# Earlier loads for the first two heads and a longer placing distance for attention in a fused attention and MLP kernel

## The chip, the cores and the metric

The kernel runs on one core of one Trainium2 chip. The metric is device time in microseconds (us) of one execution. Most executions of this kernel agree within a few tenths of a per cent, so differences of 1 us are near the noise.

Engines: PE is TensorE, ACT is ScalarE, DVE is VectorE, POOL is GpSimd, SP is SyncE.

## The reference

Eight batches of cosine attention (12 heads, 448 tokens, 64 per head), then a mixer: a low-rank token mix (rank 32) with a residual, and an MLP of 768 to 3072 to 768 with a residual.

```python
q_n = q / (np.linalg.norm(q, axis=-1, keepdims=True) + 1e-06)
k_n = k / (np.linalg.norm(k, axis=-1, keepdims=True) + 1e-06)
scores = np.matmul(q_n, k_n.transpose(0, 1, 3, 2)) / tau
attn = np.exp(scores - max); attn = attn / (sum + 1e-09)
x = (attn @ v), heads side by side            # [8, 448, 768]
h = x^T @ U @ V                               # over tokens, rank 32
u = x + h^T
out = u + np.maximum(u @ w_ch1, 0.0) @ w_ch2
```

## The kernel before

The kernel does not write its instructions in program order by hand. Every operation is an `Op` with an engine, a planned duration and what it depends on. A planner runs through all of them with its own clock and fixes the order on each engine. The engines then work through these orders, each in order, and wait where a semaphore says so. The order is therefore decided by what the planner believes about durations and landings, together with fixed priorities.

For PE work, the planner adds a distance to the end of what it depends on on another engine, and to the time at which a PSUM bank comes free:

```python
    SEM = 0.10
    SAFE = 0.25
...
    def ready_at(self, op, eng):
        t = 0.0
        for d in op.deps:
            ...
            if d.by == eng:
                t = max(t, d.start if eng == "PE" else d.end)
            else:
                t = max(t, d.end + self.SEM + (self.SAFE if eng == "PE" else 0.0))
        for s in op.acq:              # a buffer that must be free
            ...
            t = max(t, f + (self.SEM + self.SAFE if eng == "PE" else self.SEM))
```

PE takes the first operation that is ready by this, from streams in a fixed priority: transposes, batch 0's scores, attention times v, the small U and V matmuls, the other scores, and last the MLP, which fills what is left.

The loads of q and k go through POOL, which casts fp32 to bf16 on the way. All the loads below are planned to land 2.0 us after their transfer in batch 0:

```python
    def load_qk(b, h0, h1, ld=None, lo=0, uses=None):
        ld = ld or Slot(r_ld, 4 if uses is None else uses)
        ops = [load(lambda i=i, src=src: nc.gpsimd.dma_start(
            out=ld.tile[:, i, lo:lo + h1 - h0, :],
            in_=src[b, h0:h1].rearrange("h (s c) d -> s h (c d)", c=SC)),
            ..., acq=[ld], late=2.0 if b == 0 else LATE) for i, src in enumerate((q, k))]
...
    first = load_qk(0, 0, 2, uses=5)
    second = load_qk(0, 2, 4, first[0], 2)       # the same buffer
    ld, ops, _ = load_qk(0, 4, 8)
    ...
    begun = stats_first(*first[:2])              # squares, sums, 1/norm, normalized q and k
    ...
    state[0] = att(0)
```

Batch 0's first MLP starts before the token-major copy of `u` exists; six V matmuls make it on the side, each into a PSUM bank that VectorE must clear by an add, and all six are asked for at one point of the hidden loop:

```python
    def by_tokens(us, A, X):
        for i in range(3):
            for c0, c1 in ((0, CH), (CH, C)):
                mm = Slot(r_mm, 1)
                o = plan.add(Op("PE", pe_t(CH), ... V matmul ..., acq=[mm, us[i]], rel=[A]), pe_mlp)
                ... plan.add(Op("DVE", dve_t(CH), ... u = mm + X ..., deps=[o], rel=[mm, X], prio=2))
...
            if b == 0 and f == 9:
                by_tokens(us, *state["first"])
```

Of the kernel before, what the change touches and what calls it, by code (L numbers as in the profile page):

```python
# [10 lines left out]
FP = mybir.dt.float32  # L11
# [27 lines left out]


class Op:
    __slots__ = ("eng", "dur", "fn", "deps", "acq", "rel", "prio", "lat", "start", "end", "by", "seq", "fast")

    def __init__(self, eng, dur, fn, deps=(), acq=(), rel=(), prio=0, lat=0.0, fast=False):
        self.eng, self.dur, self.fn, self.prio, self.lat, self.fast = eng, dur, fn, prio, lat, fast
# [4 lines left out]
class Plan:  # L50
# [5 lines left out]
    BEGIN = {"PE": 1.0, "ACT": 2.0, "DVE": 0.9, "POOL": 1.3, "SP": 0.7}  # L56
    SEM = 0.10
    HOLD = 0.0
    SAFE = 0.25
    LAG = {"PE": 0.16, "ACT": 0.10, "DVE": 0.07, "POOL": 0.0, "SP": 0.0}  # L60

    def __init__(self):
# [7 lines left out]
        return s  # L70

    def add(self, op, stream=None):
        op.seq = self.n
        self.n += 1
        if stream is not None:
            stream.append(op)
        else:
            for e in op.eng.split("/"):
                self.loose[e].append(op)
        return op  # L80
# [5 lines that stand above are left out]
            if d.end is None:  # L86
                return None
            if d.by == eng:
                t = max(t, d.start if eng == "PE" else d.end)
            else:  # L90
                t = max(t, d.end + self.SEM + (self.SAFE if eng == "PE" else 0.0))
        new = []
        for s in op.acq:
            if s.i is not None:
                continue
            f = s.ring.free_at(new.count(s.ring))
            new.append(s.ring)
            if f is None:
                return None
            t = max(t, f + (self.SEM + self.SAFE if eng == "PE" else self.SEM))  # L100
        return t

    def run(self):
# [101 lines left out]
def kernel(  # L205
# [12 lines left out]
    nc = tc.nc  # L218

    B, H, S, D = q.shape  # L220
    C = H * D
    R = moe_U.shape[-1]
# [5 lines left out]
    SC = 4  # L228
    SCH = S // SC
# [7 lines left out]
    pool = ctx.enter_context(tc.tile_pool(name="pool", bufs=1))  # L237
# [9 lines left out]
    def ring(n, shape, dt, name, space=None):  # L247
        p = space or pool
        return Ring(n, lambda i: p.tile(shape, dt, name=name, tag=name, bufs=n))

    def fixed_ring(tiles):
# [3 lines left out]
    xn_t = fixed(3, [SCH, 12, 128], BF, "xn")  # L255
# [13 lines left out]
    r_uT = ring(1, [128, CC, 512], BF, "uT")  # L269

    w2_t = const.tile([128, NC, C], BF, name="w2_sb")
    r_relu = Ring(1, lambda i: pool.tile([128, 8 * R + S], FP, name="raw_uv", tag="relu", bufs=1)
                  if i == 0 else pool.tile([128, NC, 512], BF, name="relu", tag="relu", bufs=1))
    uv = Slot(r_relu, 3)

    def U_f():
        return uv.tile[:, 0:8 * R].rearrange("p (b t r) -> p b t r", b=2, t=4)

    def V_f():
        return uv.tile[:, 8 * R:]  # L280

    r_O = ring(3, [128, CH], FP, "O_sb")
    r_rd = ring(2, [128, 4, 1], FP, "rd")
    r_mm = ring(3, [128, 512], FP, "mm", psum)
# [48 lines left out]
    def fill(fn, n=256, prio=8, acq=(), deps=()):  # L333
        return plan.add(Op("DVE", 0.05 + n * 0.0005, fn, deps=deps, acq=acq, prio=prio))
# [49 lines left out]
# [6 lines that stand above are left out]
            (h1 - h0) * (0.31 if b else 0.35) + (1.2 if b == 0 and h0 == 4 and i == 0 else 0.0), acq=[ld], late=2.0 if b == 0 else LATE) for i, src in enumerate((q, k))]  # L390
        return ld, ops, lo

    def load_v(b, h0, h1):


        vb = v_t[b % 2]
        old = [last_av.get((b - 2, h // 2)) for h in range(h0, h1)]
        ops = []
        for hh in range(2):
            hs = slice(h0 + hh, h1, 2)  # L400
            for j in range(4):
                if j < 3:
                    lo, hi, base = 128 * j + 64 * hh, 128 * j + 64 * hh + 128, 0
                else:
                    lo, hi, base = (384, 448, 0) if hh == 0 else (0, 64, 64)
                for n, c, s0, s1 in segments(lo, hi):
                    p0 = base + n - lo
                    ops.append(load(lambda j=j, c=c, s0=s0, s1=s1, p0=p0, hs=hs:
                        nc.gpsimd.dma_start(  # L409
                            out=vb[p0:p0 + s1 - s0, hs, j, 0:D],  # L410
                            in_=v[b, hs].rearrange("h (s c) d -> c s h d", c=SC)[c, s0:s1]),
                        (s1 - s0) * (h1 - h0) * 0.001, deps=old, late=LATE if b else 2.0))
        for h in range(h0, h1):
            got[b, h, "v"] = ops
# [62 lines left out]
    def stats(b, h0, h1, ld, ops, lo, hold=()):  # L477

        pr = 0.3 + 0.03 * h0 if b == 0 else 4
        inv = Slot(r_inv, h1 - h0)  # L480
        o, _ = scales(b, h0, h1, ld, ops, lo, (0, 1), inv, pr, "DVE" if b else "ACT/DVE", hold)
        for p in range(h0 // 2, h1 // 2):
            o_ = norm(b, p, ld, lo + 2 * p - h0, inv, 2 * p - h0, {0: o, 1: o}, pr)
        return o_
# [22 lines left out]
    def norm(b, p, ld, la, inv, a, deps, pr):  # L507


        by_pe = b < PE_BATCHES  # L510
        first = b == 0 and p == 0
        xn, qkT = Slot(r_xn, 3 if first else 2 if by_pe else 1), Slot(r_qkT, 7)
        need = [xn_set[count[0] % len(xn_t)]]
        count[0] += 1

        def part(i, h0=0, h1=2):
            def fn():
                n = h1 - h0
                src = ld.tile[:, i, la + h0:la + h1, :].rearrange("p h (c d) -> p h c d", d=D)
                sc = inv.tile[:, i, a + h0:a + h1, :].unsqueeze(3).to_broadcast([SCH, n, SC, D])  # L520
                if i == 0:
                    dst = xn.tile[:, 8:12, :].rearrange("p c (h d) -> p h c d", h=2)
                else:
                    dst = xn.tile.rearrange("p b e -> p (b e)")[:, 0:9 * 128].rearrange(
                        "p (h x) -> p h x", h=2)[:, h0:h1, 0:SC * 128].rearrange(
                        "p h (c e) -> p h c e", c=SC)[:, :, :, 0:D]
                nc.vector.tensor_mul(dst, src, sc)  # L527
            return plan.add(Op("DVE", dve_t(256 * (h1 - h0)), fn, deps=need + [deps[i]], acq=[xn],
                               rel=[ld, inv], prio=pr))

        if first:
            ops = [part(0), part(1, 0, 1), part(1, 1, 2)]
            blocks = [(8, 12, ops[0]), (0, 4, ops[1]), (4, 8, ops[2])]
        else:
            ops = [part(1), part(0)]
            blocks = [(0, 8, ops[0]), (8, 12, ops[1])]
        if not by_pe:
            done = [plan.add(Op("SP", 0.1, lambda: nc.sync.dma_start_transpose(
                out=qkT.tile, in_=xn.tile.rearrange("p b e -> p (b e)")), deps=ops, acq=[qkT],
                rel=[xn], prio=0, lat=("x", 0.05 * 84, LATE)))]  # L540
        else:
            done = []
            for b0, b1, o in blocks:
                done.append(flip(
                    pe_tp, [(lambda z=z: xn.tile[:, z, :]) for z in range(b0, b1)], SCH,
                    lambda: qkT.tile, (lambda t_, x, b0=b0, b1=b1: key_tiles(t_, x, b0 // 4, b1 // 4)
                                   if b == 0 and b0 < 8 else [(t_[:, b0:b1, :], x)]),
                    [o], [qkT], [xn], 1, "ACT/DVE", 0.09 if first else 0.05, b == 0 and b0 < 8))
        got[b, p, "qkT"] = (qkT, lambda m: (done[:2] if m < 3 else done) if first else done, done)
        return ops  # L550
# [262 lines left out]
    def copy_op(op, dst, src):  # L813
        if op.by == "ACT":
            nc.scalar.copy(out=dst, in_=src)  # L815
        else:
# [1 line left out]


    xn_set = [fill(lambda t_=t_: nc.vector.memset(t_[:, 0:8, :], 0.0), 900, prio=i - 3)  # L820
              for i, t_ in enumerate(xn_t)]

    ones = 0x3F803F80

# [49 lines left out]
        last_mul.extend(muls)  # L874
        return stage0(b, X, muls)

    first = load_qk(0, 0, 2, uses=5)
    second = load_qk(0, 2, 4, first[0], 2)
    ld, ops, _ = load_qk(0, 4, 8)
    id_set = plan.add(Op("POOL", 0.8, lambda: make_identity(nc, ident)), pool_q)  # L880
    begun = stats_first(*first[:2])
    stats(0, 2, 4, *second, hold=begun)
    zf = fill(lambda: nc.vector.memset(U_f(), 0.0), 400, prio=0.1, acq=[uv], deps=begun)
    u0 = load_u(0)
    v0 = [plan.add(Op("SP", 0.45, lambda t=t: nc.sync.dma_start(out=V_f()[R * t:R * (t + 1)], in_=moe_V),
# [12 lines left out]
              plan.add(Op("POOL", 0.4, lambda: cast_u(1), deps=u1 + [z], rel=[uv]), pool_q)]  # L898
    state[0] = att(0)
    after = last_mul[-1:]  # L900
    state["first"] = prev["A"], prev["X"]
    go(1, 0, 4)
    load_w1(12, 18)
# [12 lines left out]
    for b in range(1, B):  # L916
        state[b] = att(b)
        if b + 1 < B:
            for h0, h1 in THIRDS:
                go(b + 1, h0, h1)  # L920
            load_v(b + 1, 0, 12)
    for b in range(B):
        mlp(b, *state[b])

# [39 lines left out]
```

## Time and profile before

| | before |
|---|---|
| time, median of 3 | 607.34 us |
| span of the profiled execution | 604.8 us |
| PE busy | 97% |
| first PE instruction | 7.92 us |
| last matmul run starts, lasts | 569.79, 31.27 us |

PE is so full that a table of busy shares says little. The useful reading is a ledger, which the prediction below builds with its lines: the actual start of a matmul less the unhindered time of all PE work before it is the lag that PE has gathered. Lag that grows between two points is time in which PE had nothing that it could do, or waited.

One correction to it, used from here on: a group of four small U matmuls of 384 columns takes 0.37 us in the trace, not 0.28. With this the lag of the kernel before is 19.5 us at the first long run of up-projections (start 40.6), 23.3 at 112 us and 25.0 at the last run of down-projections (start 569.8).

### The profile page before, as it was taken

How to read it: one execution, taken by the hardware profiler on the slowest of the kernel's cores; microseconds unless marked ns; L12 is line 12 of the kernel's file. 1: busy time of each engine (PE TensorE's matmuls, PEld its weight loads, DVE VectorE, ACT ScalarE, POOL GpSimd, SP SyncE). 2: the span in 40 equal slices, each digit the busy share in tenths (PEclk: the TensorE clock that was granted, in tenths of full speed). 3: DMA queues.
4: the chain of work that ended last, by engine and by line, in shares of the span. 5: the costliest groups of instructions: out<-in, count | busy, mean ns of one | idle time of the engine just before them, and what ended most of it. 6: DMA issues, size and time to landing. Idle time of an engine off the chain costs nothing.

```text
span 604.8 us, 11544 instructions
## 1 busy us (share of the span) xinstructions
PE 586.1 (97%) x4725; PEld 346.8 (57%) x4725; DVE 296.0 (49%) x714; ACT 279.5 (46%) x612; POOL 115.4 (19%) x177
## 2 busy tenths in 40 slices
PE   3899999999999999999999999999999999999997
PEld 1665666555555665666445665666545666654565
DVE  8979679989998987644711253015300210110011
ACT  6977652498782385317641077506442025014300
POOL 8246334071715326000500000000000000000000
PEclk9999999999999999999999999999999999999999
DMA  9999998999999999514902151030002110310021
GB/s 114 202 184 122 208 198 103 173 145 126 129 145 175 151 139 154 83 56 87 154 0 66 46 90 37 1 93 27 15 1 53 52 40 1 92 40 1 0 53 53
DMA packets 150164, 54.58 MB, mean 90 GB/s; under 512 B 115040, under 2 KB 150112, under 8 KB 150112
## 3 DMA queue, kind: packets, MB, share of 16 engines
q0 software_dynamic: 73344, 25.96, 38.6%
q1 hardware_dynamic: 76704, 27.86, 24.2%
q8 instruction: 37, 0.61, 0.4%
q14 instruction: 15, 0.12, 0.1%
q10 hardware_dynamic: 64, 0.02, 0.0%
HBM read 52.25 MB, written 11.01 MB: 105 GB/s over the span
## 4 chain that ended last, share of the span: by engine, by line
PE 92%; ACT 5%; DVE 2%; issue 0%; ACTq 0%
PE mm L785 36%; PE mm L751 35%; PE sc L563 9%; PE av L583 8%; ACT attn L568 3%; PE mm L675 1%; ACT qkT L815 1%; PE tp L365 1%; PE mm L640 1%; DVE ss L452 1%; PE sc L751 1%; DVE xn L527 0%; PE sc L675 0%; ACT uT L815 0%; DVE xn L820 0%
## 5 line engine op out<-in xcount | busy, mean ns | idle before, releaser
L751 PE MATMUL mm<-uT,w_sb 128*128 128x512 bf16 (+1 forms) x1134 | 236.1, 353 | 0.0
L785 PE MATMUL mm<-w_sb,relu 128*128 128x384 bf16 (+1 forms) x1368 | 233.8, 323 | 0.3 <-ACT uT L815 0.3
L568 ACT ACTIVATE attn<-sc 128x448 bf16<-128x448 f32 x336 | 161.0, 565 | 88.8 <-PE av L583 57.4
L785 PEld LDWEIGHTS <-relu 128*128 128x128 bf16 x1368 | 132.6, 98 | 86.7 <-issue 0.9
L751 PEld LDWEIGHTS <-w_sb 128*128 128x128 bf16 x1152 | 111.9, 98 | 101.1 <-issue 1.0
L774 ACT ACTIVATE relu<-mm 128x512 bf16<-128x512 f32 (+1 forms) x169 | 92.4, 547 | 149.2 <-PE mm L751 148.9
L794 DVE TENSOR_TENSOR O_sb<-mm,u_nat 128x384 f32<-128x384 f32 (+1 forms) x57 | 31.0, 547 | 227.1 <-PE mm L785 223.4
L563 PE MATMUL sc<-qkT 128*128 128x448 bf16 x336 | 103.4, 358 | 3.9 <-ACT attn L568 1.9
L583 PEld LDWEIGHTS <-attn 128*128 128x128 bf16 x1536 | 62.7, 98 | 16.0 <-DVE xn L527 0.8
L409 POOL DMA_DIRECT2D v_nat<-in_v_dram x98 | 63.2, 651 | 34.7 <-DMA w_sb<-in_moe_w_ch_dram 13.4
L583 PE MATMUL av<-v_nat,attn 128*128 128x65 bf16 x1536 | 66.6, 194 | 0.2 <-DVE X_sb L592 0.2
L452 DVE TENSOR_REDUCE ss<-sq 112x8 f32<-112x512 bf16 x96 | 63.0, 673 | 0.3
L527 DVE TENSOR_TENSOR xn<-qk_nat,inv 112x512 bf16<-112x512 bf16 (+1 forms) x97 | 62.5, 674 | 0.3
L563 PEld LDWEIGHTS <-qkT 128*128 128x128 bf16 x336 | 29.8, 98 | 24.2 <-issue 8.0
L387 POOL DMA_DIRECT2D qk_nat<-in_q_dram x25 | 17.9, 716 | 130.6 <-DVE xn L527 102.6
L592 DVE TENSOR_TENSOR X_sb<-av,rd 128x256 bf16<-128x256 f32 x96 | 40.0, 419 | 1.5
L590 DVE RECIPROCAL rd<-av 128x4 f32<-128x4 f32 x96 | 17.0, 179 | 38.2 <-PE av L583 36.7
L448 DVE TENSOR_TENSOR sq<-qk_nat 112x512 bf16<-112x512 bf16 x90 | 35.0, 408 | 0.2
L689 DVE TENSOR_TENSOR u_nat<-mm,X_sb 128x384 bf16<-128x384 f32 x36 | 19.1, 553 | 11.0 <-PE mm L675 10.8
L365 PE MATMUL tp<-ident,xn 112*128 112x112 bf16 x144 | 11.7, 226 | 10.0 <-DVE xn L527 9.5
L465 ACT ACTIVATE ln<-ss 112x32 f32<-112x32 f32 (+2 forms) x26 | 6.3, 241 | 32.7 <-DVE ss L452 32.5
L387 POOL DMA_DIRECT2D qk_nat<-in_k_dram x25 | 17.6, 703 | 5.8 <-DMA w_sb<-in_moe_w_ch_dram 5.8
(58 smaller groups left out, 160.8 us busy)
## 6 DMA issues: line engine op xcount, KB each, us to landing
qk_nat<-in_q_dram POOLq DMA_DIRECT2D x23, 224.0 KB, 5.2
qk_nat<-in_k_dram POOLq DMA_DIRECT2D x23, 224.0 KB, 6.4
w_sb<-in_moe_w_ch_dram POOLq DMA_DIRECT2D x4, 1152.0 KB, 14.3
w_sb<-in_moe_w_ch_dram POOLq DMA_DIRECT2D x8, 576.0 KB, 16.6
out_dram<-O_sb SPq DMA_DIRECT2D x15, 168.0 KB, 2.3
out_dram<-O_sb SPq DMA_DIRECT2D x16, 144.0 KB, 2.1
out_dram<-O_sb SPq DMA_DIRECT2D x16, 120.0 KB, 2.0
out_dram<-O_sb SPq DMA_DIRECT2D x16, 96.0 KB, 2.2
```

The costliest lines, as they stand in the source:

```text
L387: ops = [load(lambda i=i, src=src: nc.gpsimd.dma_start(out=ld.tile[:, i, lo:lo + h1 - h0, :], in_=src[b, h0:h1].rearrange("h (s c) d -> s ...
L409: nc.gpsimd.dma_start(out=vb[p0:p0 + s1 - s0, hs, j, 0:D], in_=v[b, hs].rearrange("h (s c) d -> c s h d", c=SC)[c, s0:s1]),
L448: nc.vector.tensor_mul(y, x, x)
L452: lambda i=i, a0=a0, a1=a1, sq=sq: nc.vector.reduce_sum(ss.tile[:, i, a0:a1, :].rearrange("p h c -> p (h c)"), sq.tile[:, 0:a1 - a0, :].re ...
L527: nc.vector.tensor_mul(dst, src, sc)
L563: nc.tensor.matmul(out=sc.tile[:, 0:S], lhsT=kT[:, 128 * m:128 * (m + 1)], rhs=qkT.tile[:, 8:12, :].rearrange("p c s -> p (c s)"), start=T ...
L568: exps[m] = plan.add(Op("ACT", act_t(S), lambda sc=sc, m=m: nc.scalar.activation(out=attn.tile[:, m, off:off + S], in_=sc.tile[:, 0:S], fu ...
L583: nc.tensor.matmul(out=av.tile[:, t, 0:D + 1], lhsT=attn.tile[:, m, 128 * t:128 * (t + 1)], rhs=v_t[b % 2][:, h, j, 0:D + 1], start=(j == ...
L592: muls.append(plan.add(Op("DVE", dve_t(256), lambda av=av, rd=rd, h=h: nc.vector.tensor_mul(X.tile[:, :, h * D:(h + 1) * D], av.tile[:, :, ...
L751: o = plan.add(Op("PE", pe_t(n), lambda cc=cc: nc.tensor.matmul(out=mm.tile[:, 0:n], lhsT=w1_sb[:, cc, f * 128:(f + 1) * 128], rhs=uT.tile ...
L774: nc.scalar.activation(out=relu.tile[:, f, 0:n], in_=mm.tile[:, 0:n], func=AF.Relu)
L785: nc.tensor.matmul(out=mm.tile[:, 0:c1 - c0], lhsT=relu.tile[:, f, i * 128:(i + 1) * 128], rhs=w2_t[:, f, c0:c1], start=(f == 0), stop=(f ...
```

## The change

The intent: the first two heads' q and k come as fp32 by the sync queue, so that POOL asks for the other heads at once; a memset of 0.48 us makes room for the first square; and for all attention from batch 1 on PE work is placed 0.8 us behind what it waits for instead of 0.25, so that small errors of the plan do not stop PE.

```diff
-    SAFE = 0.25
+    safe = 0.25
...
-        op.seq = self.n
+        op.seq, op.safe = self.n, self.safe
...
-                t = max(t, d.end + self.SEM + (self.SAFE if eng == "PE" else 0.0))
+                t = max(t, d.end + self.SEM + (op.safe if eng == "PE" else 0.0))
... (the same for PSUM banks; a wider first tile in the relu buffer; class First, which
...  gives heads 0 and 1 a place there)
     xn_set = [fill(lambda t_=t_: nc.vector.memset(t_[:, 0:8, :], 0.0), 900, prio=i - 3)
-              for i, t_ in enumerate(xn_t)]
+              for i, t_ in enumerate(xn_t[:2])]
...
-    first = load_qk(0, 0, 2, uses=5)
-    second = load_qk(0, 2, 4, first[0], 2)
+    first = lead, [plan.add(Op("SP", 0.45, lambda i=i, src=src: nc.sync.dma_start(
+        out=lead.tile[:, i], in_=src[0, 0:2].rearrange("h (s c) d -> s h (c d)", c=SC)),
+        acq=[uv], prio=-5, lat=2.5)) for i, src in enumerate((q, k))]
+    second = load_qk(0, 2, 4, uses=2)
...
+    xn_set.append(fill(lambda: nc.vector.memset(xn_t[2][:, 0:8, :], 0.0), 900, prio=0.2, deps=begun))
...
     state[0] = att(0)
     after = last_mul[-1:]
+    plan.safe = 0.8
...
+    plan.safe = 0.25
     for b in range(B):
         mlp(b, *state[b])
```

More of the change, by code (lines that the diff above doesn't have):

```diff
@@ L41 @@
 class Op:
-    __slots__ = ("eng", "dur", "fn", "deps", "acq", "rel", "prio", "lat", "start", "end", "by", "seq", "fast")
+    __slots__ = ("eng", "dur", "fn", "deps", "acq", "rel", "prio", "lat", "start", "end", "by", "seq", "fast", "safe")
     def __init__(self, eng, dur, fn, deps=(), acq=(), rel=(), prio=0, lat=0.0, fast=False):
@@ L99, in ready_at @@
                 return None
-            t = max(t, f + (self.SEM + self.SAFE if eng == "PE" else self.SEM))
+            t = max(t, f + (self.SEM + op.safe if eng == "PE" else self.SEM))
         return t
@@ L271 @@
     w2_t = const.tile([128, NC, C], BF, name="w2_sb")
-    r_relu = Ring(1, lambda i: pool.tile([128, 8 * R + S], FP, name="raw_uv", tag="relu", bufs=1)
+    r_relu = Ring(1, lambda i: pool.tile([128, 8 * R + S + 4 * SC * D], FP, name="raw_uv", tag="relu", bufs=1)
                   if i == 0 else pool.tile([128, NC, 512], BF, name="relu", tag="relu", bufs=1))
-    uv = Slot(r_relu, 3)
+    uv = Slot(r_relu, 6)
     def U_f():
@@ L279, in V_f, with tile @@
     def V_f():
-        return uv.tile[:, 8 * R:]
+        return uv.tile[:, 8 * R:8 * R + S]
+    class First:
+        slot = uv
+        @property
+        def tile(self):
+            return uv.tile[0:SCH, 8 * R + S:].rearrange("p (i h x) -> p i h x", i=2, h=2)
+    lead = First()
     r_O = ring(3, [128, CH], FP, "O_sb")
@@ L528, in part @@
             return plan.add(Op("DVE", dve_t(256 * (h1 - h0)), fn, deps=need + [deps[i]], acq=[xn],
-                               rel=[ld, inv], prio=pr))
+                               rel=[getattr(ld, "slot", ld), inv], prio=pr))
         if first:
```

## The prediction

> **What bounds the kernel now.** I read the page first, then the chain of waits in order of time, then the start of the timeline.
>
> ```profile
> PE 586.1 (97%) x4725; PEld 346.8 (57%) x4725; DVE 296.0 (49%) x714; ACT 279.5 (46%) x612; POOL 115.4 (19%) x177
> PE 92%; ACT 5%; DVE 2%; issue 0%; ACTq 0%
> ```
>
> TensorE is the bound: it is 97% busy and holds 92% of the chain. Only what is not matmul work in that chain can be won, so I list the longest of it, with four anchors of pure matmul work (columns: start, duration, what):
>
> ```profile
> 5.27 1.28 DVE ss L452 x2
> 29.07 3.49 ACT attn L568 x8
> 40.59 2.44 PE sc L751 x14
> 46.54 1.39 ACT qkT L815 x2
> 57.57 0.91 ACT qkT L815
> 99.99 1.02 ACT uT L815
> 101.05 11.86 PE mm L785 x72
> 146.38 1.42 ACT attn L568 x3
> 180.40 1.86 ACT attn L568 x4
> 222.89 2.87 ACT attn L568 x6
> 287.10 1.42 ACT attn L568 x3
> 293.60 28.06 PE mm L751 x130
> 569.79 31.27 PE mm L785 x216
> ```
>
> The chain's ACT pieces overstate the loss, because scores and matmuls still run beside them. So I keep a ledger: the order of the built program's matmuls, each at its unhindered pace in this trace. These paces are 28.06/130 = 0.216 us for a 512-column up-projection, 0.1625 for a 384-column one (130 in 21.12) and for a down-projection (48 in 7.80), 0.19 for a score, 0.032 for an attention-times-v matmul (32 in 1.02), 0.05 for a transpose. The whole order sums to 575.0 us. At each anchor the lag is actual start less summed work:
>
> - 40.6 (the first MLP's long run of up-projections; 21.1 us of work before it): lag 19.5. Of it 7.9 is the wait for the first transpose; 11.6 is lost while batch 0's attention runs, bound by VectorE and then ScalarE.
> - 101.05 (77.9 us of work): lag 23.2, so 3.7 lost in batch 1's attention.
> - 293.60 (267.8): lag 25.8, so 2.6 lost.
> - 569.79 (543.7): lag 26.1, so 0.3 lost. After it come 31.27 us of work and 3.7 us of the last add and store.
>
> So the most that a better order from batch 1 on can win is 3.7 + 2.6 + 0.3 = 6.6 us. Some of that is no wait: four small U matmuls cost about 0.09 us more than I charge, 15 groups of them 1.4 us. About 5.2 us is left. I find it in single places: after transposes near 47.2 and 58.1, where a score waits for the qkT copy (0.63 and 0.74), the uT transposes at 97 to 101 (0.48 + 0.33 + 0.49), and the four ScalarE pieces after 140 us (0.4 to 0.5 each, 1.8 together).
>
> The start, from the timeline (start, duration, engine, what, idle before and its releaser):
>
> ```profile
> 1.28 0.78 POOL L387 DMA_DIRECT2D qk_nat<-in_q_dram  x1 [0.84 <-POOLq L945]
> 4.47 0.48 DVE L820 MEMSET xn<- 112x512 uint32 x1
> 4.88 0.35 DVE L448 TENSOR_TENSOR sq<-qk_nat 112x512 bf16<-112x512 bf16 x1
> 4.93 0.63 ACT L446 ACTIVATE sq<-qk_nat 112x512 bf16<-112x512 bf16 x1 [2.91 <-DMA qk_nat<-in_k_dram]
> 7.92 0.56 PE L365 MATMUL tp<-ident,xn 112*128 112x112 bf16 x4 [7.92 <-DVE xn L527]
> ```
>
> ScalarE waits 2.91 us for the first k. VectorE does not wait: it runs memsets from 0.92 to 4.95, and its first square follows without idling. An earlier landing alone is therefore hidden by memsets.
>
> **What the Trainium skill says.** "Perfetto Trace Analysis", Identifying the Most-Contended Engine, says that matmul busy share is a poor measure of what is left. The trace agrees: 586.1 us busy hold 575.0 us of work. "VectorE: DVE Perf Modes", The perf-mode tier table, gives a two-tensor operation the 2x mode in bf16 and 1x with fp32. The trace agrees, with these two forms in the first 45 us:
>
> ```profile
> L527 DVE TENSOR_TENSOR xn<-qk_nat,inv 112x512 bf16<-112x512 bf16 x12 | 7.8, 691 | 0.1
> L448 DVE TENSOR_TENSOR sq<-qk_nat 112x512 bf16<-112x512 bf16 x10 | 3.8, 398 | 0.0
> ```
>
> The product with the fp32 inv takes 691 ns, the all-bf16 square 398. "DMA: Bandwidth & Descriptors", Specifications, gives a first-byte latency of about 1 us for loads started by GpSimd and 0.6 for the sync queue. Its section Issuing engines are not separate DMA queues says that all share 16 engines, so issuing from two saves only issue time. The trace before has no early sync-queue load; it shows 3.4 us from issue to landing for these 112 KB loads by POOL.
>
> **The change, part by part.**
>
> Load. Two POOL issues (0.78 + 0.67 us) go; the next loads of q and k, and all later ones, are issued about 1.4 us earlier. SyncE has nothing before its first load, so I put the issue near 0.9 us and landings near 3.4 (q) and 4 to 4.5 (k), estimates from the same 2 to 3.4 us that loads take to land here. One memset (0.48) moves from before the first square to after the first normalization.
>
> VectorE at the start. The memsets now end at 4.42. The square reads fp32, so it costs as the 1x product does: 0.58 instead of 0.29 in sequence. Two reduces of 0.62 end at 6.3, against 6.55. The normalization reads fp32 beside fp32 inv, 1x before and after: no change. The built order also puts the second scale-add before the first product, where before it waited 0.55 for ScalarE after it. So the first k tiles are ready near 8.8 instead of 9.44, q still near 7.8. The first transpose stays at 7.8 to 8.0.
>
> Then VectorE is given more: the q copy (0.36), the moved memset (0.48) and one half of the k copy (three copies, about 0.68), less one square (0.35) that ScalarE takes. Going on from 8.8: 0.36 + 0.27 + 0.48 + 0.68 + the old remainder of 4.5 - 0.27 - 0.35 gives pair 1's product at about 14.5 to 14.7, where it was at 13.95. The first exp comes 0.5 to 0.9 earlier (copies in parallel on two engines), but pair 1's exps stay near 18.0 (were 18.08). From there ScalarE sets the pace: 35 exps at 0.446 us are 15.6 in both; beside them before stand 1 square (0.51), three copy sets (2.7) and two small pairs (0.24), after 1 square, two sets and one single copy (2.8 in all). That saves 0.45. Against it, VectorE has two more copy sets in 16 to 30 us (1.8 us, it was 97% busy there), and ScalarE's in-order queue may wait up to 0.9 for a normalization. Sum for the start: **-0.3 us, +-1**.
>
> Distance. The number 0.8 instead of 0.25 holds for the PE work of batches 1 to 7's attention: other matmuls are put between a producer on another engine and its PE consumer. No instruction is added; the sum stays 575.0. I compared the two built orders at the paces above. A score reuses a PSUM bank of the third score before it; the work between the end of one and the start of the other is below 1.2 us in 48 of 273 cases before, in 9 after (below 0.9: 10 and 1), and the median rises from about 1.55 to 2.1. The tightest run of 12 scores has one per 0.41 to 0.55 us before, less or hardly more than an exp (0.446) with the other work of ScalarE; after it is 0.62 to 0.70. So the ScalarE backlogs at 146, 180, 223 and 287 should not build up: -1.6 of 1.8. After transposes near 47 us the next score stands 0.81 us later instead of 0.16, and at 58 us the copy has 0.57 + 0.9 us of work: -1.2 of 1.37. The uT transposes are split and mixed with down-projections: -1.0 of 1.3. From "up 384 x144" on both orders are the same, so the end costs what it did. I leave 0.2 for new waits. Sum: **-3.6 us**.
>
> Together: -3.9 of 607.34, **603.4 us**.
>
> **The rivals.**
>
> Everything in the chain goes: ACT pieces from 40 us on sum to about 14 us, so one would hope for 593. The ledger is against it, since only 6.6 us are lost there at all.
>
> The early load carries through: a 1.4 us earlier start on POOL and 0.9 us earlier exps reach the end of batch 0's attention, and with the distance this is 602. For it: copies in parallel, less ScalarE work. Against: VectorE's row of memsets, then its 97%.
>
> VectorE takes the place of the load: two more copy sets and the fp32 square delay pairs 2 to 5, costing up to 1 us, giving 604.5 to 605.
>
> The distance wins nothing, or delays attention until an MLP runs out of work: 607. For it: each dense stretch now lasts some 10 us longer, and VectorE with it. Against: 69 to 95 up-projections in a row still stand behind each attention, so none becomes the last.
>
> **Range and chances.** The distance can give 2.8 to 4.8, the start -1.3 to +1.0 around what I said, which makes 601.2 to 605.5 for 8 in 10. A 2% gain needs 12.1 us, twice what the ledger holds outside the start; a loss of 2% would need a new wait of 12 us that no order shows. Chances: 0.02 faster, 0.97 within, 0.01 slower.
>
> **What would show it.** The load right: first square of VectorE near 4.5 us and slower (about 0.6), first transpose still near 7.9, the first exp near 10.7. The start term right: the MLP's first long run near 40.3; near 39 or 42 it is wrong. The distance right: no ACT piece over 1 us in the chain after 101 us, and the lag growing by about 3 instead of 6.6 from the first MLP run to the last matmul. A score, or a first attention-times-v matmul, with TensorE idle before it at a new place would show that the distance is still too short or that ScalarE is now late for another reason. A different clock than 1.0, or missing weights at the first down-projection, would make all of it wrong.

## The result

605.34 us (604.82 to 606.38, four runs), beside 607.53 us (607.23 to 608.25, four runs) of the kernel before. The ratio is 0.9964 with a 95% interval of 0.9947 to 0.9982. Ratios here and below are the mean time of one kernel's runs over that of the other's of the same rounds, so they are not quite the ratio of the medians. The gain is real, about 2.2 us, and small: within 2%. The predicted 603.4 us asked for 3.9.

The changed kernel's profile has a span of 603.2 us; from its page the engine line and the chain:

```profile
PE 586.4 (97%) x4725; PEld 347.0 (58%) x4725; DVE 300.6 (50%) x728; ACT 276.9 (46%) x598; POOL 115.2 (19%) x175
...
PE 93%; DVE 2%; ACT 2%; POOL 1%; DMA 1%; issue 0%; ACTq 0%; POOLq 0%
```

ScalarE's share of the chain fell from 5 to 2%. That is 3 points of 600 us, or some 18 us, while the span fell by 1.6. This is the trap that the ledger is for. A share that leaves one engine goes to others: here PE has one point more, and POOL and the DMA one point each, which they did not have before.

Some pieces in the chain of waits, in order of time (start, duration, what):

```profile
9.48 5.13 DMA v_nat<-in_v_dram
...
25.34 2.50 DVE xn L536 x4
...
45.23 2.50 DVE xn L536 x4
...
51.87 0.93 DVE u_nat L734 x2
...
106.05 6.50 PE mm L794 x40
...
568.49 31.27 PE mm L794 x216
```

After 101 us no ScalarE piece is among the long ones any more: the four at 146, 180, 223 and 287 us are gone. Before that, VectorE has come into the chain, at 25 us and at 45 to 52 us. The points of POOL and the DMA are one place: up to 14.6 us the chain now follows POOL's loads and the landing of the first v, where before it followed VectorE. Experiment 6 tests what that is worth.

The ledger of both kernels, as growth of the lag:

| stretch | before | after | predicted change | measured change |
|---|---|---|---|---|
| up to the first long MLP run | 19.5 | 20.2 | -0.3 | +0.7 |
| from there to 62 us | 1.9 | 1.5 to 2.0 | -1.2 | about 0 |
| 62 to 112 us | 1.9 | 0.7 to 1.2 | -1.0 | -0.7 to -1.2 |
| 112 us to the last run | 1.7 | 0.8 | -1.6 | -0.9 |
| lag at the last run | 25.0 | 23.7 | -3.9 (with 0.2 left for new waits) | -1.3 |

The point at 62 us falls in the middle of small instructions, so it is good to 0.5 us; the sum of the two rows around it, -1.0, is sharper. After the last run, 34.7 us pass instead of 35.0. Together that is the 1.6 us of the spans.

So the distance did part of what was expected of it late in the kernel, nothing near 50 us, and the start got slower, not faster. The start first (timeline: start, duration, engine, what, idle before and what ended it):

```profile
0.74 0.39 SPq L886 DMA_DIRECT2D raw_uv<-in_q_dram  x1
...
4.28 0.63 ACT L455 ACTIVATE sq<-raw_uv 112x512 bf16<-112x512 f32 x1 [2.26 <-DMA raw_uv<-in_k_dram]
4.34 0.62 DVE L457 TENSOR_TENSOR sq<-raw_uv 112x512 bf16<-112x512 f32 x1
...
7.62 1.55 PE L374 MATMUL tp<-ident,xn 112*128 112x112 bf16 x12 [7.62 <-DVE xn L536]
...
10.62 0.63 ACT L455 ACTIVATE sq<-qk_nat 112x512 bf16<-112x512 bf16 x1 [1.14 <-DVE ss L461]
11.16 0.53 ACT L577 ACTIVATE attn<-sc 128x448 bf16<-128x448 f32 x1
```

The load came as thought (2.9 us from issue to landing for q, 3.1 for k), the square starts after the memsets and takes the longer time of fp32, the first transpose comes at 7.62 instead of 7.92 and the first exp at 11.16 instead of 11.44. The exp gains only 0.28 us, because in ScalarE's order a square stands in front of it, and that square waits 1.14 us for a reduce of VectorE. And yet the last exp of batch 0 ends at 37.85 us where it ended at 37.14. What lies between is the subject of half of the experiments.

Then the stretch at 50 to 54 us, some lines of PE, VectorE and ScalarE:

```profile
49.88 0.53 ACT L824 COPY qkT<-tp 128x448 bf16<-128x448 bf16 x1 [0.36 <-PE tp L374]
50.01 1.17 PE L730 MATMUL mm<-A_sb,V_sb 128*128 128x384 bf16 x3
50.31 0.50 ACT L783 ACTIVATE relu<-mm 128x384 bf16<-128x384 f32 x1
50.39 0.55 DVE L734 TENSOR_TENSOR u_nat<-mm,X_sb 128x384 bf16<-128x384 f32 x1
50.86 0.68 DVE L461 TENSOR_REDUCE ss<-sq 112x8 f32<-112x512 bf16 x1
...
51.78 1.02 DVE L734 TENSOR_TENSOR u_nat<-mm,X_sb 128x384 bf16<-128x384 f32 x2
52.39 0.79 PE L730 MATMUL mm<-A_sb,V_sb 128*128 128x384 bf16 x2 [0.24 <-DVE u_nat L734]
...
53.91 0.81 PE L760 MATMUL mm<-uT,w_sb 128*128 128x384 bf16 x4 [0.19 <-DVE u_nat L734]
```

Three V matmuls need 0.49 us and take 1.17 with their waits (0.16 of that is the last one's end); the fourth and fifth wait again, and so does the up-projection at 53.91. The lag grows by 1.6 us here, in two parts. The first 0.5 us are waits for ScalarE: by the semaphores in the built program the second V matmul waits for the copy at 49.88 and the third for the relu at 50.31. The kernel gives the transposes, the V matmuls and the MLP the same ring of three PSUM banks (`r_mm`), and the second V matmul is in the bank that the transposes before it filled and that this copy clears. The other 1.1 us, before the fourth and fifth V matmul and the up-projection, are waits for VectorE's adds, which have to clear banks of the ring and stand behind reduces of batch 1's statistics. Not all of it is new: before, the lag grew by 0.6 us at these V matmuls. The built orders show what has changed (runs of equal matmuls in PE's order; `tp` transposes, `sc` scores, `V` the six V matmuls):

```
before: ... tp*12 sc up ... sc up*2 V*2 sc*3 V*2 sc V sc V sc up*14 ...
after:  ... tp*8 up*11 tp*4 up*2 V*3 sc*3 tp*8 V*2 sc*2 V up*4 sc up*2 tp*4 ...
```

Before, scores stood between the V matmuls. The longer distance has moved those scores away, and what is left is V matmuls that follow each other faster than ScalarE and VectorE clear their banks.

### The profile page after: what moved, and what is told of

Same layout as the page of the kernel before. It is cut to its first block, busy times and chain, and to the rows that moved or that the text cites. A ratio compares the mean times of both kernels' runs of the same rounds, so it can differ in the third digit from the quotient of the medians.

```text
span 603.2 us, 11528 instructions
## 1 busy us (share of the span) xinstructions
PE 586.4 (97%) x4725; PEld 347.0 (58%) x4725; DVE 300.6 (50%) x728; ACT 276.9 (46%) x598; POOL 115.2 (19%) x175
## 4 chain that ended last, share of the span: by engine, by line
PE 93%; DVE 2%; ACT 2%; POOL 1%; DMA 1%; issue 0%; ACTq 0%; POOLq 0%
PE mm L794 36%; PE mm L760 35%; PE sc L572 10%; PE av L592 8%; PE mm L684 1%; PE tp L374 1%; DMA v_nat<-in_v_dram 1%; DVE xn L536 1%; PE mm L649 1%; POOL v_nat L429 1%; ACT attn L577 1%; PE sc L760 0%; POOL qk_nat L396 0%; DVE ss L461 0%; ACT qkT L824 0%
## 5 line engine op out<-in xcount | busy, mean ns | idle before, releaser
L760 PE MATMUL mm<-uT,w_sb 128*128 128x512 bf16 (+1 forms) x1134 | 241.3, 353 | 0.2 <-DVE u_nat L734 0.2
L794 PE MATMUL mm<-w_sb,relu 128*128 128x384 bf16 (+1 forms) x1368 | 231.3, 323 | 0.0
L577 ACT ACTIVATE attn<-sc 128x448 bf16<-128x448 f32 x336 | 164.6, 552 | 110.9 <-PE av L592 58.2
L783 ACT ACTIVATE relu<-mm 128x512 bf16<-128x512 f32 (+1 forms) x158 | 86.8, 549 | 129.3 <-PE mm L760 128.7
L536 DVE TENSOR_TENSOR xn<-qk_nat,inv 112x512 bf16<-112x512 bf16 x94 | 60.9, 681 | 2.4 <-DMA qkT<-xn 2.2
L457 DVE TENSOR_TENSOR sq<-qk_nat 112x512 bf16<-112x512 bf16 x87 | 33.7, 415 | 0.0
L785 DVE TENSOR_SCALAR relu<-mm 128x384 bf16<-128x384 f32 (+1 forms) x31 | 18.7, 604 | 12.8 <-PE mm L760 12.0
## 6 DMA issues: line engine op xcount, KB each, us to landing
w_sb<-in_moe_w_ch_dram POOLq DMA_DIRECT2D x4, 1152.0 KB, 14.6
```

Source lines behind the costliest of these rows:

```text
L457: nc.vector.tensor_mul(y, x, x)
L536: nc.vector.tensor_mul(dst, src, sc)
L577: exps[m] = plan.add(Op("ACT", act_t(S), lambda sc=sc, m=m: nc.scalar.activation(out=attn.tile[:, m, off:off + S], in_=sc.tile[:, 0:S], fu ...
L760: o = plan.add(Op("PE", pe_t(n), lambda cc=cc: nc.tensor.matmul(out=mm.tile[:, 0:n], lhsT=w1_sb[:, cc, f * 128:(f + 1) * 128], rhs=uT.tile ...
L783: nc.scalar.activation(out=relu.tile[:, f, 0:n], in_=mm.tile[:, 0:n], func=AF.Relu)
L794: nc.tensor.matmul(out=mm.tile[:, 0:c1 - c0], lhsT=relu.tile[:, f, i * 128:(i + 1) * 128], rhs=w2_t[:, f, c0:c1], start=(f == 0), stop=(f ...
```

## The experiments

Twelve runs, one of them the changed kernel again, all correct, each timed in four to six executions, beside nine to eleven of the kernel before on the same chip. "Lag" means the lag at the first long run of up-projections, then at the last run of down-projections.

### 1. The load alone

```diff
 (on the changed kernel)
-    plan.safe = 0.8
+    plan.safe = 0.25
```

> Only the load part (sync queue, memset moved), distance 0.25 everywhere. Theory, from the ledger of the changed kernel (lag at the first long run of up-projections 20.2 us against 19.5 before): the load part alone costs 0.7 us, so about 608.2 against 607.5 before, with that lag at 20.1 to 20.3. Rival: the start is neutral once the distance no longer depends on it (the later order takes the 0.7 back): 607.3 to 607.6. Second rival, the one of the prediction: it gains 0.3, 607.2.

Measured: 606.91 us (606.00 to 607.08), beside 606.89; ratio 0.9993 (0.9980 to 1.0006). Lag 20.2, then 24.8.

The 0.7 us at the start are there, as the theory says. In the time they do not show: after 112 us this order loses 0.7 us where the kernel before loses 1.7, with the same distance. The order between is another one, so that is a by-product. The load part by itself is worth nothing; the interval excludes a loss of the 0.7 us that I expected, and leaves a gain of up to 1.2.

### 2. The distance alone

```diff
 (on the kernel before)
     after = last_mul[-1:]
+    plan.safe = 0.8
...
+    plan.safe = 0.25
     for b in range(B):
         mlp(b, *state[b])
```

> Only the distance 0.8 for the attention of batches 1 to 7, the load as before. Theory: what the changed kernel lost at the start comes back, so 605.3 - 0.7 = 604.6 (gain 2.7 to 3.0), lag at the first long run of up-projections 19.5 and about 24.1 at the last matmul run. Rival: the two parts are not additive and it stays at 605.3. Prediction's own figure: a gain of 3.6, 603.9.

Measured: 606.30 us (605.73 to 607.68), beside 606.89; ratio 0.9988 (0.9976 to 1.0000). Lag 19.5, then 24.3.

The theory falls. With the undisturbed start, I expected 604.6; the distance alone is worth about 0.6 us. Its lag grows by 4.8 us from the first long run on, against 5.5 before and 3.5 in the changed kernel. The parts are not additive, since each edit makes the planner lay out everything after it anew. On top of the load, the distance is worth 606.91 - 605.80 = 1.1 us (the latter from experiment 5, measured in another group of runs).

### 3. The distance only from batch 2 on

```diff
         state[b] = att(b)
+        plan.safe = 0.8          # and not before the loop
         if b + 1 < B:
```

> As the kernel before, with the distance 0.8 only from batch 2's attention on. Theory: the loss of 2.95 us after 101 us falls to about 1.85 as in the changed kernel, and batch 1 keeps its 3.7: a gain of 1.1, so 606.4. Rival: the waits after 101 us stem from how batch 1 left ScalarE and do not change: 607.3. Other rival: batch 1's part of the distance is worth nothing net (its new waits at V matmuls eat it), so this does as well as distance alone, 604.6 to 605.0.

Measured: 605.74 us (605.23 to 606.51), beside 606.89; ratio 0.9978 (0.9966 to 0.9990). Lag 20.0, then 24.3; from 112 us on it grows by 0.5 us.

So the part from batch 2 on does what it was made for: 0.5 instead of 1.7 us are lost after 112 us, a gain of 1.2 in the ledger and 1.1 in the time. That is the gain of 1.1 of the theory. In batch 1 the distance brings nothing net (606.30 with it in experiment 2), which fits the last rival that I named, that the new V waits eat what it wins there, though not its 604.6 to 605.0. One more thing: the start of this kernel has the same order as the kernel before, and still its lag is 20.0 instead of 19.5. One profile differs from the next in the start.

### 4. The V matmuls apart

```diff
-            if b == 0 and f == 9:
-                by_tokens(us, *state["first"])
+            if b == 0 and f in (9, 12, 15):
+                by_tokens(us, *state["first"], (f // 3 - 3,))    # one pair at a time
```

> The changed kernel, with the six V matmuls of batch 0's tokens asked for in three pairs, three hidden blocks apart, instead of all at one point. Theory: the excess of 1.6 us that TensorE has at 50 to 54 us between these V matmuls (each waits for VectorE's add to free its PSUM bank, behind the statistics of batch 1) goes for the most part, so about 1.0 to 1.4 faster than the changed kernel, 604.1. Rival: VectorE is simply late there with everything, so the wait moves to other instructions and the time stays at 605.3.

Measured: 604.98 us (604.38 to 607.12, six executions), beside 606.89; ratio 0.9968 (0.9955 to 0.9981). Lag 23.0, then 25.9, in a profiled execution that was the slowest of the six (607.12).

From the first long run to 60 us the lag grows by 0.7 us instead of 1.5 to 1.6, so most of the V waits go. What stays is 0.5 us at the first pair, the part that waits for ScalarE. About 1 us is lost again at 100 to 107 us (the lag grows by 1.6 instead of 0.4), where batch 1's transposes and small matmuls now stand differently. Five of the six executions are at 604.4 to 605.3. Against the changed kernel (0.9964 and 0.9978 in two measurements) the difference is within the noise.

The slow execution is worth a look. Its order up to 50 us is that of the changed kernel, yet at 38 us it lags by 22.3 us instead of 19.6 (timeline, ScalarE and PE):

```profile
15.55 0.24 PE L592 MATMUL av<-v_nat,attn 128*128 128x65 bf16 x1 [1.19 <-DMA v_nat<-in_v_dram]
...
17.23 0.63 ACT L455 ACTIVATE sq<-qk_nat 112x512 bf16<-112x512 bf16 x1 [2.22 <-DMA qk_nat<-in_q_dram]
```

PE waits 1.19 us for v and ScalarE 2.22 us for the last heads' q. In the changed kernel's own profile PE waited 0.44 us at 14.33 for v, and ScalarE not at all for q. So the landing of these loads differs by more than 1 us from one execution to the next, and this start stands close behind them.

### 5. The changed kernel again

> The changed kernel once more, as the yardstick of this chip and as a second profile of its start. If the gain of 2.2 us of its first measurement holds: ratio 0.995 to 0.998, 605.0 to 605.9. If the start depends on when transfers land, the lag at the first long run of up-projections will again lie anywhere in 20 to 22.5 with the very same order (20.2 in its first profile, 22.5 in another kernel with the same start).

Measured: 605.80 us (604.95 to 606.26), beside 606.86; ratio 0.9978 (0.9965 to 0.9990). Lag 20.2, then 23.7, as in the first profile.

The two measurements, 0.9964 and 0.9978, overlap; the gain of the change is 1.1 to 2.2 us.

### 6. The first v planned later

```diff
 (on the changed kernel, the loads of batch 0's v)
-                n * (0.0055 if hs.step == 2 else 0.011)))
+                n * (0.0055 if hs.step == 2 else 0.011), late=3.5))
```

> The changed kernel, with the first v's landing planned 3.5 us after its transfer instead of 2.0; in the built order this only moves the first attention-times-v matmuls of batch 0 behind the twelve transposes of pair 1, where before 17 of them stood in front. Theory: in the changed kernel these held the transposes from 14.6 to 15.4 us until v landed, so the lag at the first long run falls from 20.2 to about 19.5 and the time by 0.7 (and by more where v lands late): ratio to before about 0.9955. Rival: VectorE, which stands in the chain from 24.7 to 30.3 us, sets the start with its additional copies: lag stays at 20.2, ratio as the changed kernel's.

Measured: 605.25 us (604.98 to 605.87), beside 606.86; ratio 0.9973 (0.9960 to 0.9985). Lag 20.3, then 23.8.

The edit did to PE what it should. The transposes of pair 1 in the changed kernel and in this one (timeline, PE):

```profile
14.33 1.25 PE L592 MATMUL av<-v_nat,attn 128*128 128x65 bf16 x15 [0.44 <-DMA v_nat<-in_v_dram]
15.39 0.94 PE L374 MATMUL tp<-ident,xn 112*128 112x112 bf16 x8
```

```profile
14.63 1.30 PE L374 MATMUL tp<-ident,xn 112*128 112x112 bf16 x12 [0.84 <-DVE xn L536]
15.73 1.97 PE L592 MATMUL av<-v_nat,attn 128*128 128x65 bf16 x32
```

The transposes come 0.76 us earlier, and the lag at the end of the start is the same. My theory falls. The exps of pair 1 began at 18.11 us here and at 18.14 there, and the second line shows why: all 32 attention-times-v matmuls stand in front of pair 1's first score in both orders. Here they come after the transposes, the score starts at 17.50, and ScalarE waits 0.95 us for it; in the changed kernel they come before and among the transposes, and the score starts at 17.65.

### 7. v and the later heads' q and k planned later

```diff
+            ..., late=(3.5 if h0 else 2.0) if b == 0 else LATE)   # q and k of heads 2 to 11
+                n * (0.0055 if hs.step == 2 else 0.011), late=3.5))
```

> As the kernel before this one, and the second and third load of q and k planned 3.5 us late too, so that ScalarE's square of the last heads stands behind pair 1's copies, not in front of them. Theory: the waits of ScalarE for the third load (0, 1.35 and 2.2 us in three profiles of this start) go; lag at the first long run 19.0 to 19.5 and a smaller spread of times; ratio to before 0.9945 to 0.9955. Rival: that wait was beside other waits, nothing more than with v alone.

Measured: 604.87 us (604.73 to 605.00), beside 606.86; ratio 0.9965 (0.9951 to 0.9979). Lag 19.6, then 23.7.

The start is back at the lag of the kernel before, and five executions lie within 0.3 us of each other instead of 1.3. Pair 1's exps begin at 18.09 as in all these starts; the last exp ends at 37.21 instead of 37.85. What is different between the two lies in ScalarE's queue, whose exps and copies from 26 us on read so, for the kernel before, the changed kernel and this one (timeline, ScalarE):

```profile
27.94 1.13 ACT L815 COPY qkT<-tp 128x672 bf16<-128x672 bf16 x3
28.84 8.30 ACT L568 ACTIVATE attn<-sc 128x448 bf16<-128x448 f32 x18
```

```profile
26.87 1.03 ACT L824 COPY qkT<-tp 128x672 bf16<-128x672 bf16 x3 [0.43 <-PE tp L374]
27.77 8.89 ACT L577 ACTIVATE attn<-sc 128x448 bf16<-128x448 f32 x19
```

```profile
28.45 1.09 ACT L824 COPY qkT<-tp 128x672 bf16<-128x672 bf16 x3
29.35 6.70 ACT L577 ACTIVATE attn<-sc 128x448 bf16<-128x448 f32 x15
```

In the changed kernel ScalarE reaches the copies of a later pair before its transposes are done, and waits 0.43 us; those transposes wait for VectorE's four products at 25.34. Then its exps come at 8.89/19 = 0.468 us instead of 0.447 (6.70/15), with short waits for scores between them. In this kernel the queue has other work first and does not wait there. Summed from start to start, the 35 exps with the waits behind them take 16.6 us in the changed kernel, and 15.5 in this one and in the kernel before. A square (0.5 us) more stands in the stretch here; the rest is the 0.6 us. It is the wait that the prediction had named as a risk ("ScalarE's in-order queue may wait up to 0.9 for a normalization") and had booked inside a sum that came out negative. Which of the two, VectorE's additional copies or ScalarE's order, one would call the cause is not separated by these runs.

### 8. A distance of 1.2

```diff
-    plan.safe = 0.8
+    plan.safe = 1.2
```

> The changed kernel with a distance of 1.2 instead of 0.8. Theory: what the distance still leaves (the lag grows by 3.5 us from the first long run to the end, by 5.5 before the change) is partly waits for ScalarE and VectorE that more room takes away: growth 2.5 to 3.0 and 0.5 to 1.0 faster than the changed kernel. Rival: what is left is the V matmuls behind VectorE at 50 to 54 us and the fixed cost of small matmuls, which no distance changes: growth 3.3 to 3.7, same time.

Measured: 618.70 us (617.34 to 619.53, four executions), beside 606.86; ratio 1.0191 (1.0174 to 1.0208). Lag 21.0, then 36.7.

Neither theory had this: 12 us slower. The ledger says where: the lag is 25.2 at 112 us and 36.0 at 131. The busy time of that stretch, for this kernel and then for the changed kernel (columns: PE, PEld, DVE, ACT, POOL busy, PEclk, DMA share, GB/s):

```profile
106.00:131.00 25.00, 17.47 (x142) 10.03 (x141) 24.58 (x61) 10.45 (x24) 6.63 (x10) 0.80 0.99 131
```

```profile
106.00:131.00 25.00, 25.00 (x199) 13.94 (x197) 23.52 (x57) 16.01 (x38) 7.29 (x11) 1.00 1.13 160
```

PE is idle for 7.5 of 25 us while VectorE is busy for 24.6. The order says why. At 0.8, PE has 40 down-projections of the first MLP left when it has done batch 1's last uT transposes, and at 0.25 it has 72; at 1.2 it has none. The first MLP has been used up as filler, the second cannot start before uT is there, and PE can only do attention, at VectorE's pace: from 104.9 to 124.9 us the chain of waits holds VectorE alone, apart from short issue gaps. And the clock: PEclk is 0.80 over the stretch and 0.50 between 122 and 126 us, so what PE still does there takes longer; by the chain that is beside VectorE's work and not the cause of the loss.

The Trainium skill has this on the page "TensorE: Matmul & The Clock Gate", section What's actually happening: the clock is at half speed when idle and needs some 3.4 us of activity to be released. This trace agrees, with 0.50 in the emptiest 4 us: the clock is at half from 119.0 to 129.3 us, and PE has been at work without a gap only from 124.95 on, 4.3 us before the release. Half idleness alone did not lower it here: between 110 and 118 us PE is busy for 4.45 of 8 us at a PEclk of 1.00.

### 9. A distance of 1.2 from batch 2 on, 0.8 in batch 1

```diff
         state[b] = att(b)
+        plan.safe = 1.2
         if b + 1 < B:
```

> The changed kernel with distance 0.8 for batch 1 as it is, and 1.2 only from batch 2's attention on. Theory of the 12 us that a distance of 1.2 cost: in batch 1 the first MLP runs out of down-projections to fill with (40 stand behind the last uT transposes at 0.8, none at 1.2), and nowhere else; here 40 stay, so no loss: 605 to 606 and lag growth from 46 us to the end of 3.2 to 3.6. Rival: a distance of 1.2 is too long as such, for every batch: 612 to 618.

Measured: 605.43 us (604.85 to 605.78), beside 606.87; ratio 0.9970 (0.9957 to 0.9984). Lag 20.7, then 24.2; growth 3.5.

No loss. The fall at 1.2 comes from batch 1 alone, where filler runs out. Nor is there a gain over 0.8: what is left after 112 us (0.8 us) is not taken away by more room.

### 10. A memset moved off VectorE

```diff
-             fill(lambda: set_v(v_t[1]), 1000, prio=3, deps=late)]
+    v_set[1] = plan.add(Op("POOL", 1.2, lambda: set_v(v_t[1], nc.gpsimd)), pool_q)
```

> The changed kernel with the five memsets of batch 1's v tile (0.6 us on VectorE near 29.6 us, in the chain there) moved to POOL. Theory: VectorE sets the end of batch 0's attention in the changed kernel, so the lag at the first long run falls from 20.2 to 19.6 or less. Rival: ScalarE sets it (it waited only 0.43 us at 26.8 for transposes that wait for VectorE) and the lag stays at 20.1 to 20.3; then the memsets only stood in the chain beside it.

Measured: 606.50 us (606.25 to 606.57), beside 606.87; ratio 0.9990 (0.9977 to 1.0002). Lag 20.3, then 25.3.

The rival holds: 0.6 us of memsets stood in the chain at 29.6 us, and taking them away moved nothing at the start. The order after it came out worse (lag growth 5.0), so this harmless edit cost what the distance had won. From 50 to 55 us alone the lag grows by 2.2 us: the V matmuls stand there as two and then four in a row. Their number is not all, for the kernel of experiment 8 has all six in a row and loses 1.3 us there. That the edit cost so much is a measure of how much the layout alone is worth: about 1 us either way.

### 11. Experiments 4 and 7 together

> v and k planned later (the version that took the start back, 19.6 at the first long run) together with the V matmuls of batch 0's tokens three blocks apart. Theory: both gains add: growth of the lag at 46 to 60 us falls from 1.6 to 0.7, so 0.5 to 0.9 faster than with the first alone: ratio to before 0.995 to 0.996. Rival: as with the V matmuls apart alone, 1 us is lost again near 105 us, because fewer down-projections (29 instead of 47) stand behind the uT transposes: same as the first alone, 0.9965.

Measured: 603.69 us (603.55 to 603.77), beside 606.87; ratio 0.9944 (0.9932 to 0.9957). Lag 19.7, then 22.4.

This beats both kernels: 3.2 us faster than the kernel before, with executions within 0.2 us. It has about the time that the prediction had for the change. The stretch at 50 us in it (timeline):

```profile
49.48 0.78 PE L730 MATMUL mm<-A_sb,V_sb 128*128 128x384 bf16 x2
...
50.49 0.73 PE L572 MATMUL sc<-qkT 128*128 128x448 bf16 x3
```

Two V matmuls, then scores and up-projections. From the first long run to 60 us the lag grows by 0.7 us, 0.5 of it at this pair. The rival's fear, fewer down-projections behind the transposes (29), did not come true: lag grows by 1.0 from 90 to 107 us and by 0.2 after 112.

### 12. The old load with the rest

The kernel before with distance 0.8 and the V matmuls four hidden blocks apart (three apart left no down-projection behind the transposes in the built order, and after experiment 8 that was not run).

```diff
+    plan.safe = 0.8              # as in experiment 2
+            if b == 0 and f in (9, 13, 17):
+                by_tokens(us, *state["first"], ((f - 9) // 4,))
```

> The load and start of the kernel before, distance 0.8 as in the change, and the V matmuls of batch 0's tokens four hidden blocks apart (44 down-projections stay behind the uT transposes). Theory: the early load is worth nothing, since the start of the kernel before has its first long run at a lag of 19.5 and the best start with the early load at 19.6 to 19.7; so this comes to a final lag of 22.3 to 22.9 and 603.5 to 604.3, ratio 0.9945 to 0.996, beside 0.9944 of the best so far. Rival: the early load does help in the timed executions (less jitter from landings): 0.5 us or more slower than the best, ratio above 0.996.

Measured: 604.88 us (604.55 to 605.98), beside 607.24; ratio 0.9964 (0.9951 to 0.9978). Lag 19.9, then 23.1.

The V matmuls apart are worth about 1.5 us on top of the distance (0.9964 against 0.9988), with most of the V waits gone: the lag grows by 0.6 us from the first long run to 62 us. The two were measured on different chips, and their intervals touch. My theory's figures were missed, 604.88 against 603.5 to 604.3 and a final lag of 23.1 against 22.3 to 22.9. Whether the early load helps is left open. The ratio is a little above 0.996, where I had put the rival, but this kernel and number 11 also differ after 112 us by 0.6 us of lag, their V matmuls are spaced differently, and the two were on different rounds; their intervals overlap. The profiled start (19.9) is no better and no worse than with the early load (19.7).

## Why the prediction was right or wrong

The interval was right: 605.34 lies in 601.2 to 605.5, near its slow end, and "within 2%" was right with the chance it got. In the second measurement (experiment 5) the gain was 1.1 us and the time, 605.80, just outside. So there is luck in the interval: the 3.9 us of gain were too many by about half or more, with both terms of the sum wrong in the same direction. By its steps:

**The bound and the ledger: right.** PE is the bound before and after, the chain's ScalarE pieces went from 5 to 2% of 600 us, and of these 18 us only 1.6 reached the span. The rival that hoped for 593 fell, as the ledger had said.

**The load: hidden, as said.** SP issued at 0.74 instead of the 0.9 that I put, landings came at 3.6 and 4.3 us, and VectorE's memsets set the first square. The square took 0.62 us as worked out from the mixed product (0.58). The first transpose came at 7.62, predicted 7.8 to 8.0. The first exp was to come 0.5 to 0.9 us earlier and came 0.28 earlier, behind the square that waited.

**The start's sum: wrong by 1.0 us, -0.3 predicted and +0.7 in the ledger.** Pair 1's product came at 13.88 as before, not at 14.5 to 14.7. What failed is the size of ScalarE's waits. From pair 1's first exp to the last exp ScalarE took 37.85 - 18.14 = 19.7 us instead of 37.14 - 18.08 = 19.1. The saving of 0.45 us of ScalarE work did arrive: start to start, its copies take 2.2 us there instead of 2.7. But the exps with the waits behind them take 16.6 instead of 15.5. The wait for a normalization, which I allowed for as "up to 0.9", is 0.43 us of that, and the exps after it were slower. Experiment 7 takes it back by the order alone. In the time, the load alone costs nothing measurable (experiment 1), since its later order happens to lose less.

**The distance: mechanism right, sum too large, -3.6 predicted.** The ledger has -2.0 from the first long run to the last. Alone it is worth 0.6 us in time (experiment 2), on top of the load 1.1. By terms:

- ScalarE's backlogs after 140 us: -1.6 predicted, -0.9 measured in the changed kernel; -1.2 where only batches 2 and up have the distance (experiment 3). No ScalarE piece over 1 us is left in the chain there, as said.
- The uT transposes near 100 us, mixed with down-projections: -1.0 predicted, -0.7 to -1.2 measured.
- The waits after transposes near 47 and 58 us: -1.2 predicted, about 0 measured. **This is the step that failed**, together with "I leave 0.2 for new waits". The scores' waits at these two places did go (0.6 and 0.7 us of lag before), but the V matmuls at 50 to 54 us now cost 1.6 us instead of 0.6, and 0.4 us more are lost between scores at 59 to 62 us. Near 47 us I had counted two up-projections and three V matmuls between the last transposes and the next score as work that fills 0.81 us. The V matmuls could not fill it: the second waits for the very copy that the score would have waited for, because that copy clears its bank, and the third for a relu. That is 0.5 us where the score had waited 0.6. The other 1.1 us are waits for VectorE's adds. The order that I had before me showed three V matmuls in a row, then two, then one, where before scores stood between them. Experiments 4, 11 and 12 put them apart, and the growth up to 60 us falls to 0.6 to 0.7 us, of which 0.5 is the wait for ScalarE at the first pair.

**The rival "delays attention until an MLP runs out of work"** did not come at 0.8, since 40 down-projections stayed behind. It came in full at 1.2. I had looked at the up-projections behind each later attention, where there is room, and not at the first MLP, whose filler fell from 72 to 40 by this very change.

**What stays open:** which part of the start's 0.6 us is due to VectorE's additional copies and which to ScalarE's order; whether the early load is worth anything in a kernel that has the rest; and what the moved memset does alone, since no run parts it from the load.

## What to carry to other kernels

When work is moved apart to hide waits, look at what fills the room: a filler that needs a buffer which a busy engine must clear is a wait of its own, and a filler that is used up leaves a hole, which here cost 12 us at 1.2 where 0.8 had gained 1 to 2. Keep a ledger of unhindered work against actual starts; here ScalarE's fallen share of the chain, read as time, overstated the gain tenfold. In a planned order each edit lays out everything after it anew, worth about 1 us either way here, so measure a part of that size alone and together before giving it credit, and plan loads with the landing that they have, not the best one.

## What the Trainium skill lacked or had wrong

- "VectorE: DVE Perf Modes", section The TRN2 errata, gives 691 ns for an fp32 two-tensor operation of 512 elements. The mixed bf16 and fp32 product takes that (691 ns in the group of the kernel before). The one fp32 square on VectorE, which reads one tensor twice, took 0.62 us. That is no proof against the page: the bf16 square at the same place took 0.35 us where its group's mean is 398 ns, so the place can account for it.
- "DMA: Bandwidth & Descriptors", section Specifications, compares the two queues by first-byte latency, about 1 us and 0.6 us. The page does not compare them from issue to landing. Measured from issue to landing, the two early fp32 loads of 224 KB by the sync queue took 2.9 and 3.1 us, and the casting loads of half the size by POOL 3.4 us before the change and 4.0 beside these.
- No page that I read says how far landings vary between executions of the same order. ScalarE's wait for the same load of q was 0, 0.65 and 2.22 us in three profiles with the same start.
- "Perfetto Trace Analysis" advises occupancy and gaps, and has no word on counting filler. Here 72, 40 and 29 down-projections in reserve behind batch 1's uT transposes went with 607, 605 and 604 us, and none with 619.
